# A new written-out order of the same instructions on all engines, and of the buffers they use (Mamba-2 SSD, then a SiLU feed-forward block)

## The chip, the cores and the metric

The kernel runs on one core of a Trainium2 chip. The metric is the time of one execution on the device in microseconds (us). An engine is named as in the profile: PE is TensorE, the matrix unit, and PEld its weight loads; DVE is VectorE, ACT is ScalarE, POOL is GpSimd, SP is SyncE, which only issues transfers here.

## The reference

Two stages run one after the other. The first is a chunked state-space scan over 4 batches x 8 heads of 768 steps, with 32 channels and 16 states per head; `a` is the decay of each step, `x`, `B` and `C` are the inputs. The second is a feed-forward block with SiLU on the result, seen as 3,072 tokens of 256 numbers.

```python
# scan, for each chunk; cum = cumsum(log a) within the chunk
M = einsum('bhin,bhjn->bhij', Cc, Bc) * exp(cum_i - cum_j) * causal
y = einsum('bhij,bhjd->bhid', M, xc) + einsum('bhin,bhnd->bhid', Cc, state) * exp(cum)
state = exp(sum(la)) * state + sum_j(Bc_j x xc_j * exp(cum_last - cum_j))
# feed-forward: x (3072, 256), w_in (256, 2048), w_out (2048, 256)
h = x @ w_in
out = (h / (1 + exp(-h))) @ w_out
```

## The kernel before, in words

**Tiling.** The sequence is cut into 12 units of 256 steps (three per batch, numbered `u` = 0 to 11), each worked as four chunks of 64 steps. Two units make a pair `G` of 512 tokens, on which the feed-forward block works. The 2,048 hidden features are 8 groups of 256 (`i` or `j`). Weight tile `n` is group n of `w_in` for n under 8 and group n - 8 of `w_out` above.

**Two ways to multiply.** Pair 0 is multiplied in plain fp32 (`s`, line 667, and `n`, line 735). Pairs 1 to 5 use the faster fp32r format with each operand split into a high part and two corrections, `h`, `l` and `d`, so three cheaper products stand in for one (line 776 for the first matmul, 757 for the second). The weights are first rounded on the device from their raw bits, by ACT, DVE and an integer addition on POOL, and then split; the last step of the split is a transfer that accumulates onto its destination, issued from POOL (line 322).

**The order is written out by hand.** `SCHEDULE` (lines 18 to 96) is a list of tokens. Each names a step and its indices, and a loop at the end of the kernel calls the steps in that order:

```python
for tok in line.split():
    f, *q = tok.split(",")
    DO[f](*map(int, q))
```

A step emits instructions for one engine, or a transfer. So the list fixes the order of instructions on every engine and in every queue, and each engine works through its own in that order; one that waits holds back all behind it on the same engine. Between engines only data and buffers order the work. `SLOTS` (lines 98 to 112) says which physical buffer each new tile takes, out of 49 small ones (`s2k`), 12 large ones (`r4k`), 7 for raw weights and split activations (`raw`) and 3 banks of PSUM (`hp`).

**The steps that the prediction speaks of.**

| token | engine, line | what it does |
|---|---|---|
| `z` | PE 404, 406 | dummy matmuls at the start |
| `ip`, `ia`, `ir`, `lw,n`, `Ln`, `Lt`, `Lx`, `La`, `Lp` | mostly SP 338 to 346, 277, 243, 251, 258, 218, 226 | loads of decays, raw weights, B and C (two layouts, tiles `bn` and `tbc`), x, and the tables `az` (to `ab`) and `ac` (to `pz`) |
| `AA`, `AD` | POOL 425, 431, 433 | clip the decays and write them to the tables `az` and `ac` in DRAM, which `La` and `Lp` read back broadcast |
| `ab,u,k`, `tp,u` | PE 467, 496 | transposes at the start |
| `E,u,k` | DVE 477 | scan that makes the decay matrix of half `k` of a unit |
| `P,u`, `P01` | DVE 449, 442 | scan of the prefix products |
| `T,u,i` | DVE 490 | transposes B (`bh`, i = 0) or C (`ct`, i = 1) |
| `ce,u`, `C,u` | ACT 511; POOL or DVE 516 | C for the two parities of heads; C times the prefix (`cw`) |
| `B,u` | POOL 485 | B times the decays to the chunk's end |
| `g0,u`, `gd,u` | PE 550, 536 | the products C B and B x, in the PSUM banks `ga` and `gb` |
| `b,u,c` | ACT 559 | evacuates the B x products |
| `M,u,w` | DVE 565 | C B times the decay matrix |
| `S,u,t`, `SM,u` | DVE 578, 580; ACT 588 | the state from chunk to chunk; its copy for the matmul |
| `Y,u` | PE 601, 610 | the unit's output: within the chunk (needs `M`), from the state (needs `SM` and `cw`) |
| `y`, `xh`, `x,u,0`, `x,u,1` | ACT 643, 649; DVE 624, 627 | evacuate `Y` and split it into `h`, `l`, `d` |
| `u,n`, `v,n`; `w,n,*`; `W,n` | ACT 283, 286; DVE 292, 296, 299; POOL 310 | round weight tile n |
| `H`, `Wl`, `Wd`; `Wm`, `We` | ACT 314, 318; POOL 322 | split weight tile n; the accumulating transfers for its `l` and `d` |
| `s,u,j`, `si`; `n` | PE 667, ACT 673; PE 735 | first and second matmul of pair 0 |
| `a,G,i`, `ax`, `d,G,i`, `dg` | PE 776, ACT 787, PE 776, ACT 797 | first matmul of pair G: `h` and `l` products, a scaling, `d` product, SiLU |
| `h`, `l`, `e` | ACT 803, DVE 624, 627 | split the result |
| `f,k` | PE 757 | the next k matmuls of the second product, from a list that `e` fills (12 per group) |
| `Va`, `Vd`, `Vt`, `o`, `O`, `ot`, `or`, `os` | ACT, DVE, PE, SP 763, 769, 697, 685, 689, 709, 715, 717, 720 | evacuate, transpose and store a pair |

The buffers that tie units together: `ab` and `xt` exist twice (unit u and u + 2 share one), `pz`, `tbc`, `bn`, `pfx`, `ct`, `bh`, `ce`, `cw` and `sm` once. `ga` and `gb` serve `g0`, `gd`, `Y` and, in turn, the first matmul of the pairs (even groups `ga`, odd ones `gb`).

## Time and profile before

| | us |
|---|---|
| runs of the kernel before | 335.66, 335.91, 340.67; median 335.91 |
| the profiled execution | 338.26, of which its span 336.4 |
| busy: PE, DVE, ACT, POOL | 322.3, 226.6, 216.6, 79.9 |
| idle time of PE with a named wait | 10.2 in eleven waits, the longest 1.8 |
| bytes moved by the DMA engines | 35.03 MB, mean 104 GB/s |
| DMA share by 8-us stretches, 8 to 40 and 80 to 104 us (no unit) | 0.96 to 1.14 |

The span is the time from the first to the last instruction of the profiled execution; the rest of its time lies around it. Durations below come from this one execution, and sums are made against it. A busy engine is one with an instruction in flight: a matmul's end is modelled, so busy PE time may hold small pauses, which show only in the times from start to start. Idle time of an engine other than PE costs nothing by itself; it matters where PE waits for what that engine has not yet done. A DMA share is the mean busy share of the core's 16 DMA engines, and can read a little over 1 in a short stretch.

### The profile page before, as it was taken

The page shows a single profiled execution, that of the slowest core. Times are in us where ns is not written, and L with a number is a line of the kernel's source. Part 1 is how long each engine was busy: PE and PEld are TensorE (multiplying, and loading weights), DVE is VectorE, ACT ScalarE, POOL GpSimd, SP SyncE. Part 2 cuts the span into 40 slices and gives each one's busy share as a digit, 9 for nine tenths or more (in the row PEclk, how much of TensorE's full clock was granted, in tenths as well). Part 3 has the DMA queues.
Part 4 walks back from the last instruction along what each step waited for, and adds up shares of the span by engine and source line. Part 5 has one row for each costly group of instructions (what it writes and reads, how often), then busy time and mean ns, then how long its engine had stood idle before and what let it go on. Part 6 is the DMA issues. An engine that isn't in the chain of part 4 may idle for free.

```text
span 336.4 us, 7603 instructions
## 1 busy us (share of the span) xinstructions
PE 322.3 (96%) x3086; PEld 245.5 (73%) x3086; DVE 226.6 (67%) x314; ACT 216.6 (64%) x340; POOL 79.9 (24%) x96
## 2 busy tenths in 40 slices
PE   7799999988999999999999999999999999999994
PEld 3578746664667878886887888778887888888883
DVE  4995998569525974858596499775656933737473
ACT  3589988674599777574763775655667655375431
POOL 2286765828451641100030020000000000000000
PEclk9999999999799999999999999999999999999998
DMA  7999869997998896232342162262000320004002
GB/s 182 180 323 255 222 152 256 231 172 134 236 189 133 160 188 111 71 56 37 80 104 51 25 144 43 43 126 35 2 0 2 55 33 2 0 0 72 0 0 62
DMA packets 98129, 35.03 MB, mean 104 GB/s; under 512 B 80352, under 2 KB 87264, under 8 KB 98096
## 3 DMA queue, kind: packets, MB, share of 16 engines
q1 hardware_dynamic: 90960, 25.71, 34.4%
q0 software_dynamic: 4784, 8.59, 14.1%
q10 hardware_dynamic: 2352, 0.26, 0.5%
q8 instruction: 24, 0.39, 0.5%
q14 instruction: 9, 0.07, 0.1%
HBM read 22.81 MB, written 3.34 MB: 78 GB/s over the span
## 4 chain that ended last, share of the span: by engine, by line
PE 82%; DVE 7%; SPq 4%; DMA 4%; issue 2%; ACT 1%; POOL 0%; ACTq 0%; DVEq 0%; POOLq 0%
PE hp L757 27%; PE gb L776 16%; PE ga L776 16%; PE o_ps L757 5%; PE hp L667 5%; PE hp L735 5%; DMA tbc<-in_B_dram 3%; DVE ab L477 2%; PE ga L610 1%; DVE st L580 1%; PE ga L601 1%; PE ga L550 1%; SPq L251 1%; PE ga L536 1%; DVE ab L565 1%
## 5 line engine op out<-in xcount | busy, mean ns | idle before, releaser
L757 PE MATMUL hp<-r4k,s2k 128*128 128x512 f32 x400 | 112.4, 393 | 0.0
L757 PEld LDWEIGHTS hp<-r4k,s2k 128*128 128x128 f32 x400 | 74.4, 188 | 16.3 <-issue 0.3
L624 DVE SCALAR_TENSOR_TENSOR r4k<-r4k,r4k 128x1024 fp32r<-128x1024 f32 x40 | 49.5, 1240 | 31.1 <-ACT r4k L803 30.0
L627 DVE SCALAR_TENSOR_TENSOR r4k<-r4k,r4k 128x1024 fp32r<-128x1024 f32 x40 | 48.5, 1218 | 31.3 <-ACT r4k L803 21.6
L776 PE MATMUL ga<-raw,s2k 128*128 128x512 f32 x240 | 62.7, 396 | 2.0 <-ACT r4k L673 1.2
L776 PE MATMUL gb<-raw,s2k 128*128 128x512 f32 x240 | 61.7, 392 | 0.0
L776 PEld LDWEIGHTS ga<-raw,s2k 128*128 128x128 f32 x240 | 44.8, 188 | 13.9 <-issue 1.6
L776 PEld LDWEIGHTS gb<-raw,s2k 128*128 128x128 f32 x240 | 44.7, 188 | 10.5 <-ACT gb L787 0.6
L803 ACT ACTIVATE r4k<-r4k 128x1024 fp32r<-128x1024 f32 x40 | 41.5, 1054 | 0.5 <-DVE r4k L627 0.4
L322 POOL DMA_DIRECT2D s2k<-s2k x32 | 31.4, 1206 | 30.5 <-ACT s2k L318 12.0
L787 ACT ACTIVATE ga<-ga 128x1024 f32<-128x1024 f32 x20 | 20.2, 1010 | 22.6 <-PE ga L776 22.6
L787 ACT ACTIVATE gb<-gb 128x1024 f32<-128x1024 f32 x20 | 20.2, 1010 | 22.2 <-PE gb L776 22.2
L735 PE MATMUL hp<-r4k,s2k 128*128 128x512 f32 x64 | 31.5, 628 | 0.0
L757 PE MATMUL o_ps<-r4k,s2k 128*128 128x512 f32 x80 | 31.0, 393 | 0.0
L797 ACT ACTIVATE r4k<-ga 128x1024 f32<-128x1024 f32 x20 | 20.5, 1025 | 16.2 <-PE ga L776 15.6
L667 PE MATMUL hp<-r4k,s2k 128*128 128x256 f32 x128 | 29.6, 383 | 0.0
L310 POOL TENSOR_TENSOR s2k<-s2k,s2k 128x512 uint32<-128x512 uint32 (+1 forms) x19 | 27.4, 1454 | 6.3 <-DVE s2k L296 4.3
L667 PEld LDWEIGHTS hp<-r4k,s2k 128*128 128x128 f32 x128 | 23.8, 190 | 4.9 <-issue 0.9
L485 POOL TENSOR_TENSOR BT<-bn,ab 128x256 f32<-128x256 f32 x10 | 9.0, 899 | 74.5 <-DVE ab L477 58.3
L477 DVE TENSOR_TENSOR_SCAN ab<-ab,diag 128x512 f32<-128x512 f32 x20 | 25.1, 1257 | 0.0
L797 ACT ACTIVATE r4k<-gb 128x1024 f32<-128x1024 f32 x20 | 20.5, 1025 | 5.6 <-PE gb L776 3.8
L735 PEld LDWEIGHTS hp<-r4k,s2k 128*128 128x128 f32 x64 | 12.4, 199 | 12.8 <-issue 11.3
(118 smaller groups left out, 385.3 us busy)
## 6 DMA issues: line engine op xcount, KB each, us to landing
s2k<-s2k POOLq DMA_DIRECT2D x32, 256.0 KB, 6.2
ab<-az SPq DMA_DIRECT2D x20, 256.0 KB
raw<-in_moe_w_in_dram SPq DMA_DIRECT2D x8, 512.0 KB
raw<-in_moe_w_out_dram SPq DMA_DIRECT2D x8, 512.0 KB
out_dram<-r4k SPq DMA_DIRECT2D x44, 64.0 KB
xt<-in_x_dram SPq DMA_DIRECT2D x20, 128.0 KB
pz<-ac SPq DMA_DIRECT2D x10, 130.0 KB
bn<-in_B_dram SPq DMA_DIRECT2D x20, 64.0 KB
```

The source lines that it names most:

```text
L310: nc.gpsimd.tensor_tensor(out=dst[:, :, fs].bitcast(U32), in0=u[:, :, fs], in1=v[:, :, fs], op=ALU.add)
L322: nc.gpsimd.dma_start(out=f32(WK[n, p]).rearrange("p k f -> p (k f)"), in_=other.rearrange("p k f -> p (k f)"), accum_op=ALU.add)
L477: nc.vector.tensor_tensor_scan(out=o, data0=src, data1=diag.rearrange("p h t -> p (h t)"), initial=0.0, op0=ALU.mult, op1=ALU.add)
L624: nc.vector.scalar_tensor_tensor(out=l, in0=f32(h), scalar=BACK, in1=y, op0=ALU.mult, op1=ALU.add)
L627: nc.vector.scalar_tensor_tensor(out=d, in0=f32(h), scalar=-(BACK + 1.0), in1=y, op0=ALU.mult, op1=ALU.subtract)
L667: nc.tensor.matmul(out=hp[:, i], lhsT=WT[j][:, kc, 128 * i:128 * i + 128], rhs=XM[:, 2 * kc:2 * kc + 2, u], start=(kc == 0), stop=(kc == K ...
L735: nc.tensor.matmul(out=NP["o"][m], lhsT=WT[8 + f // 2][:, f % 2, 128 * m:128 * m + 128], rhs=GT[0, f // 2][:, f % 2], start=(f == 0), stop ...
L757: nc.tensor.matmul(out=ACC[P, 2 * (p == "d") + m], lhsT=WK[8 + f // 2, p][:, f % 2, 128 * m:128 * m + 128], rhs=rhs, start=(f == 0 and p ! ...
L776: nc.tensor.matmul(out=o, lhsT=WK[j, q][:, kc, 128 * i:128 * i + 128], rhs=xs[:, 2 * kc:2 * kc + 2], start=(start and q == "h" and kc == 0 ...
L787: nc.scalar.activation(t, t, AF.Copy, scale=1.0 + Z)
L797: nc.scalar.activation(g, t, AF.Silu, scale=BACK)
L803: nc.scalar.activation(t, GT[G, i], AF.Copy, scale=-LESS * Z)
```

## The change

Only `SCHEDULE` and `SLOTS` change: all 77 lines of the first and the lists of the second. Every step is still called once with the same indices, except that the `n` and `f` steps are cut into other portions. The code of the steps is the same, and so are the line numbers. The order was searched for with a model of the engines and transfers; it was found with transfers of two queues sharing the DMA engines, and GpSimd's early dispatch of its next instruction, in the model. The diff below shows the lines around the places that the prediction speaks of: the start, units 2 and 3, unit 4, unit 7, and the buffer lists.

```diff
-ch ci Ln,0,0,0,1 ip,0,0 cI Ln,0,0,1,1 c1 cp cP ia,1 z,1 z,1 z,1 P01,0,0 P01,0,1 z,0,6 lw,0 z,0,6 z,0,6 ia,0 A
-ab,1,1 Ln,1,0,0,0 ce,0,1 ip,1,0 B,0,1 Ln,1,0,1,0 E,0,0 v,2 E,1,1 Ln,1,1,1,0 Lx,1,1,0 B,0,0 ce,0,0 tp,0 D,0 S,0,0 w,2,0
-tq,0 ir,0 g0,0 Lx,1,0,0 S,0,1 ab,1,0 M,0,1 tp,1 ce,1,0 ce,1,1 lw,1 S,0,2 tq,1 E,1,0 SM,0,1 ir,2 C,0 M,0,0 P01,1,0
-w,2,2 lw,4 SM,0,0 B,1,1 B,1,0 w,2,1 Y,0 X0,0,0 X0,0,1 W,2,2,0 P01,1,1 S,0,3 w,0,2 D,1 S,1,0 W,2,2,1 u,1 W,0,2,0 g0,1
...
-s,0,3 w,9,1 si,1,4 W,8,1,0 Wd,1 H,3 s,1,3 ce,2,0 Lp,2,0 w,11,0 w,10,1 AD,1 n,1 W,10,1,0 si,0,3 v,5 E,2,0 n,1 T,3,1
-H,4 M,2,0 W,11,1,0 Wd,4 P,2 b,2,0 Ln,3,0,1,0 Wl,0 w,7,2 H,9 n,1 b,2,1 Lx,3,0,0 S,2,0 Lt,3,0,1,0 w,7,1 n,1 u,6 Lp,3,0
-S,2,1 M,2,1 W,5,1,0 s,0,5 C,2 Lt,3,0,2,0 S,2,2 Ln,3,0,0,0 Lx,3,1,0 Wl,2 SM,2,0 v,6 SM,2,1 w,6,0 Wm,0 E,3,0 u,12 n,1
...
-w,13,2 u,13 Wm,11 Lt,5,1,0,0 xh,3 x,3,0 We,0 s,1,5 W,12,1,0 w,13,0 n,2 Wm,3 T,4,0 ce,4,0 Wm,9 si,1,5 Wl,5 a,1,0 v,15
-E,4,0 E,4,1 x,3,1 u,15 w,15,2 Wd,8 Lp,4,0 We,3 ax,1,0 s,1,7 B,4 ce,4,1 d,1,0 Lx,4,0,0 H,12 Ln,5,0,1,0 S,3,3 n,1 si,1,7
-n,1 w,13,1 dg,1,0 P,4 g0,4 Lt,5,1,3,0 w,14,2 W,13,1,0 gd,4 n,1 H,6 La,5,1,0 n,2 b,4,0 Lt,5,1,2,0 M,4,1 M,4,0 C,4 S,4,0
-w,14,1 Wd,11 b,4,1 S,4,1 We,4 Wd,9 S,4,2 SM,4,1 SM,4,0 Y,4 We,2 Wm,5 y,4,0 n,1 y,4,1 Ln,5,0,0,0 W,14,1,0 Lx,5,0,0 H,7
...
-f,1 Vd,1,0 Lt,8,1,2,0 Vd,1,1 B,7 f,1 Lx,7,1,0 f,2 dg,2,2 f,2 g0,7 gd,7 e,2,1 b,7,0 f,1 M,7,0 Lt,8,0,2,0 T,8,1 f,1
-Lx,8,0,0 Ln,8,0,1,0 x,6,0 ce,8,1 f,1 b,7,1 f,2 o,1,0,2 f,1 h,2,2 f,1 M,7,1 a,2,4 Lx,8,1,0 S,7,0 S,7,1 ax,2,4
...
+ch ip,0,0 cI ci z,1 z,1 z,1 Ln,0,0,0,1 P01,0,0 Ln,0,0,1,1 z,0,6 z,0,6 z,0,6 lw,0 ia,0 c1 z,1 ia,1 cp z,1 z,1 z,1 z,1
+Ln,1,1,0,0 tq,0 ab,1,1 ce,0,1 lw,1 ce,0,0 g0,0 Ln,1,1,1,0 B,0,1 v,2 E,1,1 ip,1,0 ir,3 B,0,0 v,1 D,0 ab,1,0 C,0
+Lx,1,0,0 u,1 w,2,0 tp,1 S,0,0 B,1,1 Lt,3,1,0,0 M,0,1 ce,1,1 E,1,0 S,0,1 Lx,1,1,0 M,0,0 S,0,2 SM,0,1 w,2,1 w,2,2 SM,0,0
+B,1,0 tq,1 P01,1,0 Y,0 S,0,3 P01,1,1 D,1 ce,1,0 S,1,0 w,0,2 w,1,0 X0,0,0 lw,3 X0,0,1 lw,10 W,2,2,0 lw,4 S,1,1
+Lt,3,1,2,0 S,1,2 g0,1 M,1,1 ir,0 W,2,2,1 ir,1 s,0,2 w,1,1 M,1,0 ir,2 lw,9 Lt,3,1,1,0 W,0,2,0 w,1,2 lw,8 Lt,3,1,3,0
+W,0,2,1 u,3 co s,0,0 v,3 SM,1,1 C,1 SM,1,0 S,1,3 Ln,2,1,0,0 si,0,2 Y,1 w,3,0 u,10 W,1,2,0 v,4 W,1,2,1 Ln,2,1,1,0
...
+W,3,1,0 s,0,4 AA,1 H,4 si,0,4 ca Lx,3,1,0 lw,11 La,2,0,0 w,9,1 s,1,4 tp,2 Lt,3,0,1,0 w,8,1 u,5 s,1,3 si,0,1 Lt,3,0,3,0
+Wd,2 W,8,1,0 si,1,4 Lx,2,1,0 v,10 n,1 tq,2 si,1,3 w,5,0 AD,0 v,5 n,1 u,11 n,1 ce,2,1 E,2,1 W,9,1,0 n,1 v,6 H,8 n,1
+v,11 lw,7 w,5,1 Lx,2,0,0 AD,1 H,1 ce,2,0 E,2,0 w,5,2 B,2 Lt,3,0,2,0 w,11,0 Lt,4,1,1,0 n,1 s,0,3 u,7 v,7 g0,2 u,6
+Lp,2,0 Wl,0 w,7,0 w,10,2 W,10,1,0 gd,2 W,5,1,0 Wl,4 P,2 w,11,1 H,3 La,3,1,0 La,3,0,0 b,2,0 n,1 C,2 n,1 E,3,0
+Ln,3,0,0,0 n,1 si,0,3 lw,15 S,2,0 ce,3,1 b,2,1 w,11,2 Wl,3 S,2,1 lw,12 M,2,0 Wl,8 H,10 Lt,3,0,0,0 s,0,5 lw,14 Wd,8 H,5
+M,2,1 n,1 S,2,2 Wl,10 w,7,1 si,0,5 Wm,0 SM,2,1 E,3,1 Wd,5 W,11,1,0 n,2 Lt,4,1,0,0 SM,2,0 H,9 Wl,2 Y,2 Ln,3,0,1,0
+Lp,3,0 w,7,2 W,7,1,0 We,0 w,6,0 Lx,3,0,0 u,12 La,4,0,0 lw,13 n,1 y,2,1 Wd,4 Wl,1 B,3 w,6,1 Wm,1 T,3,0 ce,3,0 Wm,4
...
+s,1,5 x,2,1 E,4,0 Ln,4,0,0,0 Ln,4,0,1,0 y,3,1 y,3,0 S,3,3 xh,3 x,3,0 a,1,0 x,3,1 Wl,9 si,1,5 ax,1,0 T,4,1 w,15,0 E,4,1
+n,2 Lx,4,1,0 u,13 We,1 ce,4,0 H,12 B,4 Wm,5 w,13,2 w,14,2 w,13,0 Lp,4,0 T,4,0 w,14,0 d,1,0 w,13,1 ce,4,1 Wl,11 w,14,1
+n,1 dg,1,0 s,1,7 Wd,3 g0,4 gd,4 M,4,1 W,13,1,0 Wm,9 P,4 Wd,12 Lt,5,1,0,0 h,1,0 W,14,1,0 Lx,5,0,0 b,4,0 La,5,1,0 si,1,7
+C,4 Lt,5,0,0,0 AD,2 b,4,1 M,4,0 n,1 S,4,0 Lt,5,1,2,0 S,4,1 S,4,2 Wl,7 n,3 Wd,7 SM,4,0 Lp,5,0 n,1 We,8 SM,4,1 Y,4 y,4,0
...
+g0,7 b,7,0 P,7 Lt,8,0,0,0 f,1 Lt,8,1,0,0 M,7,0 f,1 b,7,1 h,2,2 f,1 h,2,3 M,7,1 f,1 Lt,8,1,3,0 f,1 S,7,0 Ln,8,0,0,0
+l,2,1 e,2,2 S,7,1 f,2 a,2,4 f,1 Lt,8,0,3,0 Lt,8,0,1,0 f,2 Lt,8,0,2,0 Lx,8,1,0 T,8,0 C,7 ax,2,4 a,2,5 ax,2,5 l,2,2
...
 SLOTS = {
     "s2k": """
-7 10 19 30 2 22 4 5 8 26 6 0 3 1 9 11 12 13 14 15 16 17 18 20 21 23 24 25 27 28 29 31 32 33 34 35 36 37 38 39 40
...
+4 11 23 35 0 22 3 6 8 27 7 1 5 2 9 10 12 13 14 15 16 17 18 19 20 21 24 25 26 28 29 30 31 32 33 34 36 37 38 39 40
...
     "raw": """
-0 1 2 3 4 5 6 1 0 2 3 4 6 1 5 2 6 3 0 4 0 5 1 2 6 3 0 4 5 1 2""",
+0 1 2 3 4 5 6 1 0 2 6 3 5 1 2 4 6 3 0 1 2 4 5 6 3 0 1 2 4 6 5""",
     "hp": """
-0 1 2 0 1 2 0 2 1 0 2 1 0 2 1 0 1 2 0 1 2 2 2 2 2 2 2 1 0 2 0 1 2 0 1 2 0 1 2 0 1""",
+0 1 2 0 1 2 2 0 1 2 1 0 2 0 2 0 2 1 0 2 2 2 2 2 2 2 2 0 1 2 1 0 2 1 0 1 0 2 1 0 2""",
```

## The prediction

> **What bounds the kernel now.** I read the page first: the span, the busy times and the granted clock over the 40 slices.

> ```profile
> span 336.4 us, 7603 instructions
> PE 322.3 (96%) x3086; PEld 245.5 (73%) x3086; DVE 226.6 (67%) x314; ACT 216.6 (64%) x340; POOL 79.9 (24%) x96
> ...
> PEclk9999999999799999999999999999999999999998
> ```

> TensorE (PE) is busy 96% of the span, VectorE (DVE) and ScalarE (ACT) about two thirds each, and one slice near 85 us runs at a lower clock. Every engine issues the same instructions in a new order, so the work of TensorE cannot shrink; only its pauses can move. I added up that work: 128 matmul records of L667 at 0.216 us, 64 of L735 at 0.43, 480 each of L757 and L776 at 0.227 (start to start, read off the timeline), and for each sequence unit about 2.4 us of small matmuls (L536, L550, L601, L610). From the first L667 at 19.12 us to the last L757 at 330.7 this gives 298.6 us of work in 311.6 us, so about 13 us are pauses or slow clock. Some 4 of these are 0.1-us hitches, most of them between small and large matmuls, which stay in any order.

> The waits of TensorE come next. Each row gives engine, tile, line, what it waited for, and then total us, times, longest.

> ```profile
> PE ga L601 <- DVE ab L565: 1.8, 1, 1.8
> PE ga L610 <- ACT sm L588: 1.7, 1, 1.7
> PE ga L536 <- issue: 1.3, 1, 1.3
> ...
> PE ga L776 <- ACT r4k L673: 1.2, 1, 1.2
> PE ga L776 <- ACT bxs L559: 0.7, 1, 0.7
> ```

> The first is the start of the kernel (16.4 us). The other four are the whole of what a new order could win after that, and the timeline says why three of them occur.

> ```profile
> 61.57 10.05 DMA tbc<-in_B_dram
> ...
> 71.64 0.66 DVE L490 STREAM_TRANSPOSE bh<-tbc 128x256 f32<-128x256 f32 x1 [2.07 <-DMA tbc<-in_B_dram]
> 72.14 2.28 DVE L477 TENSOR_TENSOR_SCAN ab<-ab,diag 128x512 f32<-128x512 f32 x2
> 74.34 0.67 DVE L627 SCALAR_TENSOR_TENSOR raw<-raw,ys 128x512 fp32r<-128x512 f32 x1
> ```

> (First line from the chain of work that ended last, the others from the timeline.) Here VectorE stands at `T,4,0` until a 10-us transfer lands, then does both scans `E,4`, and only then `x,3,1` (L627), which TensorE's `d,1,0` needs. TensorE idles from about 73.7 to 75.1 (the wait names ACT, but this operand came last).

> ```profile
> 80.59 2.77 DVE L580 SCALAR_TENSOR_TENSOR st<-st,pfx,bxs 128x64 f32<-128x64 f32 x2
> 80.99 2.27 POOL L310 TENSOR_TENSOR s2k<-s2k,s2k 128x512 uint32<-128x512 uint32 x1
> 83.39 0.69 ACT L588 ACTIVATE sm<-st,par 128x128 f32<-128x128 f32 x2 [2.44 <-DVE st L580]
> ```

> The second of the two small updates `S,4,1` and `S,4,2` lasts until GpSimd's addition `W,14` (L310) ends; the same form takes 0.28 us elsewhere. So `SM,4` is late, and `Y,4` stops TensorE for 1.7 us. Right behind it the clock drops.

> ```profile
> 83.00:84.00 1.00, 0.00 (x0) 0.00 (x0) 0.97 (x3) 0.61 (x2) 1.00 (x3) 1.00 1.19 249
> ...
> 86.00:87.00 1.00, 1.00 (x2) 0.34 (x1) 0.00 (x0) 0.97 (x3) 1.00 (x2) 0.50 1.11 252
> ```

> (Columns: stretch, its length, busy us of PE, PEld, DVE, ACT, POOL, then clock, DMA share, GB/s.) The L735 matmuls from 84.9 to 88.8 start 0.35 to 0.43 us later than their 0.43 rhythm, about 2.2 us in all.

> **The change part by part.** All counts per engine are unchanged (2,111 program rows on PE, 316 on DVE, 345 on ACT, 101 on POOL, 227 on SP), so nothing is added or removed; every term is a wait.

> *Start, 0 to 25 us.* The chain to `Y,0` is the same. One more dummy matmul (0.43 us) stands ahead of `ab,0,1`, which puts the first scan 0.4 us later; `S,0,2` now stands behind `M,0,0`, which gives back about 0.1. In `Y,1`, `C,1` now stands behind `w,1,2`, 0.68 us later, with little cover: about 0.5. Sum +0.8; bounds 0 (other work in front is also lighter) and +1.5.

> *Units 2 and 3, 36 to 60 us.* This is the part that the trace of before cannot show. The `ac` table of unit 2 (`AD,0`) moves behind `AA,1`, `W,3` and `W,8` on GpSimd; before, it was issued at 27.5. `W,8` needs `w,8,1`, which VectorE reaches at about 33 to 36 (it had done as much work by 35.9 before). So `AD,0` is issued at 36 to 38 and lands at 41 to 43 (the page's 4.6 us for `ac<-r4k`). SP stands at `Lp,2` until then, with `La,3,1` and `La,3,0` behind it (2 x 256 KB), and VectorE stands at `P,2` and then `E,3,0` for them. I take 44 to 46 for `P,2`. Behind it come `w,11,1`, `C,2`, `E,3,0`, three `S`, `w,11,2`, two `M`, `w,7,1`, `E,3,1`, `w,7,2`: 7.9 us by their rows, 6.9 with the 0.08 us by which neighbours overlap, 1.6 for two GpSimd additions that hold VectorE up, then `W,7` on GpSimd (1.5). That is 10.0 us to `s,0,7`, which TensorE reached at 54.56 and, with the same work in front, reaches at 55.4 now. So `P,2` may start as late as 45.4. I take +0.5; bounds 0 and +5.7 (below).

> *`x,3,1`.* In the new order it stands ahead of `T,4,1`, `E,4,1` and `T,4,0`. The sum of VectorE's rows in front of it falls from 47.8 to 44.4 us; `d,1,0` comes only 0.9 us earlier in TensorE's work. The wait of 1.4 us goes: -1.4. What is late next is `E,4,0`, which now stands in front of `x,2,1`'s followers and waits for `La,4`; that is issued once `Y,2` has ended (about 54), and 10 us to land, as in the row above, still ends at 64, when VectorE gets there.

> *`Y,4` and the clock.* 5.3 us of TensorE's work now lie between `g0,4` and `Y,4`, against 3.6 before. VectorE needs `M`, `P`, `M` and three `S` in that time, 2.9 us, and ACT 0.7. `W,13` and `W,14` still run there and may hold VectorE for up to 2.3 us. I count the 1.7 as gone but leave +0.5 for that: -1.2. With the pause the slow clock goes: -2.2. Bounds for the two: 0 and -3.9. [...]

> *`a,2,4`, 155.7 us.* The evacuation `b,7,1` stood on ACT behind `ce,8,1`, which waited for `T,8,1` on VectorE. Now `b,7,1` follows `b,7,0`, and `M,7,1` follows `M,7,0`. The pause of 1.1 us goes: -1.1.

> *Weights.* `lw,4` moves behind `lw,3` and `lw,10` (1 MB), `w,4,0` and `w,4,1` behind nine other VectorE steps; `W,4` then ends at about 31.4, `s,0,4` needs it at 32.4. The accumulating transfers (L322) land 6.2 us after issue; the one with the least time, `We,4` behind `W,15`, is issued at about 84, and `d,1,4` comes at about 99. Both hidden: 0; if the 1 us at `s,0,4` is gone, up to +1.

> *The hitch at 58.4 us* (1.3 us, "issue", inside `gd,3`) has no releaser in the profile. I leave it: 0; bounds -1.3 and +1.3.

> *The other 170 us.* The order of the large matmuls differs by at most 4 us of work anywhere. Before had one pause there; I allow +0.6 for new ones, bounds 0 and +2.

> The tail is the same chain of L697, L709, L717 and L720 with the same 18 matmuls behind `e,5,7`: 0.

> Sum: +0.8 +0.5 -1.4 -1.2 -2.2 -1.1 +0.6 = **-4.0 us**. The profiled execution took 338.26 us with a span of 336.4; it would become 334.3. It is 2.35 us above the median of the runs, 335.91, so the predicted median is 331.9, say **332**.

> **The rivals.**

> *The late table.* If `Lp,2` or `La,3` needs 10 us to land (the row of `tbc<-in_B_dram`) after an issue at 41, `P,2` or `E,3,0` starts at 51 and `s,0,7` at 61.0 in place of 55.4: 5.7 us, and a pause of that kind brings the half clock, 2.2 more. In place of the +0.5 that is +7.9: -4.5 + 7.9 = +3.4, so 339.3. It decides from `P,2` later than 45.4, and the kernel gets slower than before from about 48. For it: the DMA engines are busy at 0.75 to 1.1 in these 20 us, and one issue of `pz` took 4.6 us. Against it: before used the same bytes in the same time, and SP has 0.35 MB less to carry before `Y,2` than it had.

> *Given back to the DMA engines.* Summed over the stretches of the windows up to 128 us, the DMA engines are busy 119 us. If units 5 to 7 are paced by their loads, TensorE runs ahead by 4 us and waits for them: only the 1.1 at 155.7 and about 1 more stays, some 334.5 to 336. For it: VectorE already waited 2.7 us for `ab<-az` at 96.4. Against it: TensorE had no wait between 89 and 153 us, and shares of 0.49 at 72 to 80 and 0.66 at 104 to 112. This is also the case in which the two effects that the order was searched with are not those that held TensorE.

> *More than forecast.* Start at 0, the hitch gone, `Y,4` free: -1.4 -1.7 -2.2 -1.1 -1.3 = -7.7, so 328.2.

> **How the numbers follow.** Forecast (329.3 to 334) 0.50; given back or cancelled (334 to 337.5) 0.22; late table 0.18, half of it dearer than worked out because VectorE is full there and later units follow; more than forecast 0.10. Within 2% (6.7 us, about what a measurement of this kernel can tell from no change) lie 329.2 to 342.6. Faster by over 2%: 0.10. Slower by over 2%: 0.13, from the dearer part of the late table and pauses that I have not seen. Within: 0.77. The range is 328.5 to 340.5: it takes in the late table's price and most of the larger gain.

> **What would show it.** Right: no wait of L776 for `x,3,1` near 73 and of `sm` near 82, clock 1.0 from 80 to 90, no pause at 156, and `a,1,2` at about 83 to 85 in place of 88.8. The late table: VectorE idle before L449 or L477 between 43 and 52 with a DMA as releaser, and TensorE waiting at L610 or L667 near 55. Given back: waits of VectorE for `ab<-az` or `tbc` between 80 and 130 with TensorE idle behind them. The prediction is wrong if a pause of over 2 us opens anywhere that I counted as unchanged, above all if the clock falls with it.

## The result, and the profile after

The changed kernel takes 333.95 us (median of 20 runs, 330.77 to 336.51); the kernel before, run beside it, 339.8 us (20 runs, 335.17 to 342.09). The ratio is 0.988, interval 0.984 to 0.992: a little faster, inside the 2% that the prediction called "within". The forecast was 332.0 us against 335.91, a ratio of 0.988 too. (The ratios here count only the runs of a kernel within 1.5% of its fastest; the medians count all.) The three runs shown before were a low draw: in 120 runs of the kernel before, taken in the course of this study, the median was 339.2 us and the standard deviation 2.6. By medians the change brings 5.9 us, 1.7%. The profiled execution took 332.88 us in place of 338.26: -5.4, where the sum said -4.0.

The head of the changed kernel's page (span; busy time, share and instructions of each engine; granted clock in 40 slices; shares of the chain that ended last):

```profile
span 330.8 us, 7604 instructions
PE 320.5 (97%) x3086; PEld 245.9 (74%) x3086; DVE 227.7 (69%) x314; ACT 217.2 (66%) x340; POOL 76.7 (23%) x96
...
PEclk9879999999999999999999999999999999999998
...
PE 95%; DVE 1%; DMA 1%; SPq 1%; ACT 0%; issue 0%; ACTq 0%; DVEq 0%
```

The drop near 85 us is gone; two stretches at half clock stand at the start of the kernel, in the second and third slices (7.9 to 11.3 us and 18.2 to 21.6 us). TensorE is 95% of the chain (82% on the page of before), so almost nothing else is left on it. The waits of TensorE, the same view as before:

```profile
PE ga L601 <- DVE ab L565: 1.8, 1, 1.8
PE o_ps L416 <- DVE s2k L412: 1.5, 1, 1.5
PE o_ps L404 <- DVE s2k L351: 1.4, 1, 1.4
PE ga L550 <- ACT ce L511: 0.8, 1, 0.8
PE gb L709 <- DVE r4k L697: 0.5, 1, 0.5
```

Four of the waits that were shown of before are gone: `sm` at L610, the "issue" at L536, and L776 for `r4k` and for `bxs`. What remains is the start of the kernel (the first four rows, all in the first 30 us) and the tail (the last row); between them no wait with a named releaser is left. Around unit 4 (timelines of VectorE, GpSimd and ScalarE in the changed kernel: start, duration, engine, line):

```profile
69.40 0.68 DVE L627 SCALAR_TENSOR_TENSOR raw<-raw,ys 128x512 fp32r<-128x512 f32 x1
...
73.96 0.64 DVE L490 STREAM_TRANSPOSE bh<-tbc 128x256 f32<-128x256 f32 x1
...
77.17 1.59 POOL L310 TENSOR_TENSOR s2k<-s2k,s2k 128x512 uint32<-128x512 uint32 x1
...
79.84 1.04 DVE L580 SCALAR_TENSOR_TENSOR st<-st,pfx,bxs 128x64 f32<-128x64 f32 x3
80.92 0.69 ACT L588 ACTIVATE sm<-st,par 128x128 f32<-128x128 f32 x2 [1.39 <-DVE st L580]
```

`x,3,1` (L627) runs at 69.4 in place of 74.3, `T,4,0` at 74.0 with no wait in front of it. GpSimd's addition ends at 78.8, ahead of the three `S` updates, which take 1.04 us together, and `sm` is written from 80.9. TensorE starts `Y,4` at 81.85 without a pause, and the clock stays (windows, columns as before):

```profile
80.00:84.00 4.00, 4.00 (x104) 2.32 (x102) 2.88 (x6) 1.28 (x4) 4.00 (x6) 1.00 0.68 134
84.00:88.00 4.00, 4.00 (x17) 2.76 (x16) 0.00 (x0) 2.73 (x6) 3.94 (x5) 1.00 1.11 214
```

**Where the time went.** To add this up I give each execution a lateness: the start of a step's first matmul, minus the durations of all TensorE work that stands in front of it in that kernel's order, at the rates of the prediction. It grows only where TensorE pauses or runs slowly. The first column is the lateness at the first `s` of the second half (`s,1,0`), each next one its growth up to the step named, all in us of the profiled execution.

| execution | start | to `a,1,0` | to `d,1,0` | to `Y,4` | to `a,1,2` | to `g0,7` | to `a,2,4` | to `a,5,0` | sum |
|---|---|---|---|---|---|---|---|---|---|
| before | 7.0 | 1.9 | 1.8 | 0.4 | 3.2 | 1.6 | 1.1 | 2.4 | 19.3 |
| changed | 8.3 | 0.6 | -0.1 | 0.7 | -0.2 | 2.1 | 0.1 | 2.3 | 13.8 |
| b_b71 | 8.9 | 0.5 | 6.9 | 1.8 | 0.3 | 1.5 | 0.2 | 2.3 | 22.3 |
| b_x31 | 9.3 | 0.4 | 0.2 | 5.9 | -0.1 | 2.3 | 1.1 | 2.4 | 21.5 |
| b_t40 | 6.7 | 1.3 | 5.6 | 2.4 | 0.2 | 1.5 | 1.1 | 2.4 | 21.1 |
| b_three | 8.4 | 0.6 | 0.3 | 1.4 | -0.3 | 1.6 | 0.2 | 2.3 | 14.4 |
| b_w14 | 10.1 | 0.4 | 6.5 | 2.3 | -0.3 | 3.1 | 1.1 | 2.4 | 25.5 |
| b_lt | 8.4 | 0.4 | 0.9 | 0.4 | 1.6 | 1.6 | 1.1 | 2.3 | 16.6 |
| b_thin | 7.3 | 0.4 | 0.3 | 0.5 | 3.2 | 1.5 | 1.1 | 2.4 | 16.6 |
| b_lw | 8.1 | 0.5 | 1.2 | 0.4 | 1.6 | 1.5 | 1.1 | 2.4 | 16.8 |
| b_five | 10.4 | 1.7 | 0.2 | 0.5 | 0.0 | 3.2 | 0.2 | 2.3 | 18.5 |
| a_p2 | 6.9 | 1.6 | -0.1 | 0.7 | -0.3 | 1.7 | 0.2 | 2.4 | 13.1 |
| a_t40 | 10.2 | 0.6 | -0.1 | 0.7 | -0.2 | 3.1 | 0.1 | 2.4 | 16.8 |
| a_lw | 7.0 | 0.7 | -0.1 | 0.7 | -0.3 | 3.4 | 0.1 | 2.3 | 13.8 |

The names from the third row on are the experiments below (`b_` starts from before, `a_` from the changed kernel). Changed minus before gives -5.5, the -5.4 of the profile. The start differs from execution to execution of one and the same order by nearly 4 us, and no experiment touches it, so single executions must be read column by column, and times by their medians. With ten to twelve runs and a standard deviation near 2 us, a median is known to some 0.8 us, so a term of 1 us is seen in the columns and hardly in the times. The column "to `g0,7`" varies too, from 1.5 to 3.4 in executions of both orders, and no experiment explains it.

### The profile page after: what moved, and what is told of

The parts are those of the page before. It is cut to its first block, busy times and chain, and to the rows that moved or that the text cites. A ratio compares the mean times of both kernels' runs of the same rounds, so it can differ in the third digit from the quotient of the medians.

```text
span 330.8 us, 7604 instructions
## 1 busy us (share of the span) xinstructions
PE 320.5 (97%) x3086; PEld 245.9 (74%) x3086; DVE 227.7 (69%) x314; ACT 217.2 (66%) x340; POOL 76.7 (23%) x96
## 4 chain that ended last, share of the span: by engine, by line
PE 95%; DVE 1%; DMA 1%; SPq 1%; ACT 0%; issue 0%; ACTq 0%; DVEq 0%
PE hp L757 28%; PE ga L776 17%; PE gb L776 17%; PE hp L667 9%; PE hp L735 9%; PE o_ps L757 6%; PE ga L550 2%; PE ga L610 2%; PE ga L601 2%; PE gb L601 1%; PE ga L536 1%; DMA s2k<-in_a_dram 1%; PE gb L550 1%; PE hp L467 1%; DVE ab L565 0%; PE gb L610 0%
## 5 line engine op out<-in xcount | busy, mean ns | idle before, releaser
L757 PE MATMUL hp<-r4k,s2k 128*128 128x512 f32 x400 | 112.5, 393 | 0.0
L757 PEld LDWEIGHTS hp<-r4k,s2k 128*128 128x128 f32 x400 | 74.4, 188 | 16.3 <-issue 0.5
L776 PE MATMUL ga<-raw,s2k 128*128 128x512 f32 x240 | 62.8, 397 | 0.0
L776 PE MATMUL gb<-raw,s2k 128*128 128x512 f32 x240 | 62.5, 396 | 0.0
L627 DVE SCALAR_TENSOR_TENSOR r4k<-r4k,r4k 128x1024 fp32r<-128x1024 f32 x40 | 49.0, 1230 | 17.7 <-ACT r4k L803 8.6
L776 PEld LDWEIGHTS ga<-raw,s2k 128*128 128x128 f32 x240 | 44.7, 188 | 11.5 <-issue 1.0
L776 PEld LDWEIGHTS gb<-raw,s2k 128*128 128x128 f32 x240 | 44.7, 188 | 11.3 <-issue 1.2
L322 POOL DMA_DIRECT2D s2k<-s2k x32 | 29.5, 1207 | 18.2 <-DMA s2k<-s2k 11.6
L757 PE MATMUL o_ps<-r4k,s2k 128*128 128x512 f32 x80 | 31.3, 397 | 0.0
L735 PE MATMUL hp<-r4k,s2k 128*128 128x512 f32 x64 | 30.4, 600 | 0.0
L667 PE MATMUL hp<-r4k,s2k 128*128 128x256 f32 x128 | 30.3, 388 | 0.0
L477 DVE TENSOR_TENSOR_SCAN ab<-ab,diag 128x512 f32<-128x512 f32 x20 | 24.4, 1221 | 7.6 <-DMA ab<-az 7.6
L667 PEld LDWEIGHTS hp<-r4k,s2k 128*128 128x128 f32 x128 | 24.4, 194 | 6.5 <-issue 2.2
L797 ACT ACTIVATE r4k<-gb 128x1024 f32<-128x1024 f32 x20 | 20.5, 1026 | 10.8 <-PE gb L776 8.0
L310 POOL TENSOR_TENSOR s2k<-s2k,s2k 128x512 uint32<-128x512 uint32 (+1 forms) x19 | 24.0, 1273 | 15.5 <-DVE s2k L299 9.3
L318 ACT ACTIVATE s2k<-s2k 128x512 fp32r<-128x512 f32 x32 | 19.4, 629 | 0.0
```

The costliest lines, as they stand in the source:

```text
L310: nc.gpsimd.tensor_tensor(out=dst[:, :, fs].bitcast(U32), in0=u[:, :, fs], in1=v[:, :, fs], op=ALU.add)
L322: nc.gpsimd.dma_start(out=f32(WK[n, p]).rearrange("p k f -> p (k f)"), in_=other.rearrange("p k f -> p (k f)"), accum_op=ALU.add)
L477: nc.vector.tensor_tensor_scan(out=o, data0=src, data1=diag.rearrange("p h t -> p (h t)"), initial=0.0, op0=ALU.mult, op1=ALU.add)
L627: nc.vector.scalar_tensor_tensor(out=d, in0=f32(h), scalar=-(BACK + 1.0), in1=y, op0=ALU.mult, op1=ALU.subtract)
L667: nc.tensor.matmul(out=hp[:, i], lhsT=WT[j][:, kc, 128 * i:128 * i + 128], rhs=XM[:, 2 * kc:2 * kc + 2, u], start=(kc == 0), stop=(kc == K ...
L735: nc.tensor.matmul(out=NP["o"][m], lhsT=WT[8 + f // 2][:, f % 2, 128 * m:128 * m + 128], rhs=GT[0, f // 2][:, f % 2], start=(f == 0), stop ...
```

## The experiments

Theory: three places in the order of the steps held TensorE up, VectorE's at `x,3,1` and at `S,4`, ScalarE's at `b,7,1`; with each step moved, its share of the gain appears. Rival: the loads of unit 4 land late whatever stands in front, because the DMA engines are full, so moving steps on VectorE moves the loss.

**One part alone, and all three.** Each is the kernel before with one step moved.

```diff
# b_w14: w,14,1 behind the state updates and their copies
-S,4,0 w,14,1 Wd,11 b,4,1 S,4,1 We,4 Wd,9 S,4,2 SM,4,1 SM,4,0 Y,4
+S,4,0 Wd,11 b,4,1 S,4,1 We,4 Wd,9 S,4,2 SM,4,1 SM,4,0 w,14,1 Y,4
# b_x31: x,3,1 ahead of T,4,0 and the scans
-Wm,3 T,4,0 ce,4,0 Wm,9 si,1,5 Wl,5 a,1,0 v,15 E,4,0 E,4,1 x,3,1 u,15
+Wm,3 x,3,1 T,4,0 ce,4,0 Wm,9 si,1,5 Wl,5 a,1,0 v,15 E,4,0 E,4,1 u,15
# b_b71: b,7,1 ahead of ce,8,1
-x,6,0 ce,8,1 f,1 b,7,1 f,2
+x,6,0 b,7,1 ce,8,1 f,1 f,2
# b_three: all three moves
```

> The kernel before with one step moved: w,14,1 (VectorE, L296) stands behind SM,4,0, so that the addition W,14 on GpSimd (L310) can only start behind S,4,1 and S,4,2. Theory (the addition stretched the small updates, that made the pause at Y,4, and the pause made the slow clock): the two S take about 0.3 us each in place of 2.77 together, the wait of L610 for sm (1.7 us) is gone, the clock stays at 1.00 from 80 to 90 us, a,1,2 starts at about 85.0 in place of 88.8, and the execution is 3.9 us shorter. Rival 1 (the slow stretch does not hang on the pause): the clock is 0.50 somewhere between 80 and 90 all the same, and only 1.7 us are won. Rival 2 (W,14 is late now): a new wait of L776 opens between 90 and 110 us and the gain is given back. In the part before 60 us nothing is changed: if the hitch of 1.3 us inside gd,3 near 58 us belongs to this order, it is there again.

> The kernel before with x,3,1 (VectorE, L627) moved ahead of T,4,0, nothing else. Theory: the wait of L776 in d,1,0 (1.4 us near 73.5) is gone, d,1,0 starts at about 73.7 in place of 75.1, and TensorE stays 1.4 us ahead: -1.4 us. Rival (Y,4 is paced by the transfer tbc that lands at 71.6, by T,4,0 and by the scans behind it, which do not come earlier): TensorE reaches Y,4 1.4 us earlier and waits 1.4 us longer there (3.1 us in place of 1.7), and nothing is won, or, if the longer pause lengthens the slow clock, up to 1.7 us is lost. The hitch inside gd,3 near 58 us is there again if it belongs to this order.

> The kernel before with b,7,1 (ACT, L559) moved ahead of ce,8,1, nothing else. Theory: the wait of L776 in a,2,4 near 155.7 us (1.1 us between the 757 and the 776 matmuls) is gone and nothing takes its place: -1.1 us in the profile, too little for the times. Rival: ce,8,1 comes no later, but M,7,1 behind T,8,1 holds the other bank, so the wait moves on to a,2,5 and 0.5 us or more of the 1.1 stays. The hitch inside gd,3 near 58 us is there again if it belongs to this order.

> The kernel before with the three single moves together (w,14,1 behind SM,4,0; x,3,1 ahead of T,4,0; b,7,1 ahead of ce,8,1). Theory (three pauses with three causes of their own): the gains add, 3.9 + 1.4 + 1.1 = 6.4 us, so the profile is as short as that of the changed kernel or shorter (about 330 to 332.5 us), though only three of about 1,400 steps are moved. Rival (Y,4 is paced by the load and not by TensorE): the 1.4 us come back as a pause at Y,4, -5.0 us at most, and the slow clock can return with it (-2.8).

Measured, beside a before of 340.5 us: b_w14 340.9 (ratio 1.007, 1.001 to 1.013), b_x31 340.7 (0.998, 0.995 to 1.002), b_b71 340.0 (1.001, 0.995 to 1.007). Not one of them gains what its term said in the times. b_three gives 334.9 (0.979, 0.972 to 0.987), but in four runs only, one of which is still at 340.1. The trace of b_b71, which differs from before only at 156 us, shows what hides the single gains (timeline of VectorE, then windows):

```profile
77.15 0.64 DVE L490 STREAM_TRANSPOSE bh<-tbc 128x256 f32<-128x256 f32 x1 [7.16 <-DMA tbc<-in_B_dram]
77.64 2.27 DVE L477 TENSOR_TENSOR_SCAN ab<-ab,diag 128x512 f32<-128x512 f32 x2
79.83 0.67 DVE L627 SCALAR_TENSOR_TENSOR raw<-raw,ys 128x512 fp32r<-128x512 f32 x1
```

```profile
72.00:76.00 4.00, 2.29 (x11) 1.64 (x9) 0.00 (x0) 2.42 (x4) 0.86 (x1) 1.00 1.27 217
76.00:80.00 4.00, 0.00 (x0) 0.00 (x0) 2.85 (x4) 0.00 (x0) 0.00 (x0) 0.59 0.58 110
```

The same chain as in the profile of before, but the load of `tbc` lands 5.5 us later: VectorE stands 7.2 us, TensorE does nothing from 76 to 80 us, and the granted clock falls (mean 0.59 in these 4 us, 0.56 in the next). The column "to `d,1,0`" is 6.9 here and 1.8 in the first profile of before: this one place differs from execution to execution by more than the whole forecast. At `a,2,4` b_b71 has 0.2 in place of 1.1, so that term is right, and too small for a median to show.

In b_x31, `x,3,1` no longer waits, and the loss appears one step further (timelines of VectorE and TensorE):

```profile
74.95 0.70 DVE L490 STREAM_TRANSPOSE bh<-tbc 128x256 f32<-128x256 f32 x1 [4.02 <-DMA tbc<-in_B_dram]
...
80.99 5.49 PE L735 MATMUL hp<-r4k,s2k 128*128 128x512 f32 x6 [1.63 <-POOL s2k L310]
```

`d,1,0` is in time (0.2), but 5.9 us go before `Y,4`: VectorE stood 4 us at `T,4,0`, the `n` matmuls wait for an addition on GpSimd behind it, and the clock is halved from 80.28 to 87.11. Moving `x,3,1` alone does not save the time. b_three's profiled execution had its load at 72.45, and the three columns are as the theory has them (0.3, -0.3, 0.2), with 1.4 up to `Y,4`, 0.8 of it the same wait for the addition.

**Does the place of `T,4,0` matter at all?** It was tried from both sides, with the load of its last tile issued earlier as a third test.

```diff
# b_t40: before, T,4,0 behind the scans and x,3,1
-Wm,3 T,4,0 ce,4,0 Wm,9 si,1,5 Wl,5 a,1,0 v,15 E,4,0 E,4,1 x,3,1 u,15
+Wm,3 ce,4,0 Wm,9 si,1,5 Wl,5 a,1,0 v,15 E,4,0 E,4,1 x,3,1 T,4,0 u,15
# a_t40: the changed kernel, T,4,0 back ahead of x,3,1
-a,1,0 x,3,1 Wl,9 ... w,13,0 Lp,4,0 T,4,0
+a,1,0 T,4,0 x,3,1 Wl,9 ... w,13,0 Lp,4,0
# b_lt: before, the load Lt,4,0,3 ahead of La,4,0
-La,4,0,0 ... La,4,1,0 Lt,4,0,3,0
+Lt,4,0,3,0 La,4,0,0 ... La,4,1,0
```

> The kernel before with T,4,0 (VectorE, L490) moved behind E,4,0, E,4,1 and x,3,1, nothing else. In the profiles so far with the order of before, T,4,0 started at 71.6, 77.2 and 77.9 us, each time when its load landed, and TensorE stood at d,1,0 for 1.4, 6.3 and 5.9 us. Theory (VectorE standing at T,4,0 in front of x,3,1 is what makes the kernel before slow and uneven): no wait of L776 at d,1,0; a landing as late as 78 costs only the 1 to 2 us by which g0,4 is late; no slow clock between 76 and 85; the times lose their upper half (most below 339) and the median falls by 3 to 4 us. Rival (the load ab of E,4,1, 256 KB, issued right before on the same queue, lands just as late): VectorE now waits at L477 for ab<-az as long as it did at L490, x,3,1 behind it is as late, and the times stay as they are.

> The changed kernel with T,4,0 put back ahead of x,3,1, nothing else. Theory (the place of T,4,0 on VectorE is the core of the gain): x,3,1 waits for the landing of tbc, somewhere from 70 to 75 us; d,1,0, which starts at 72.3 in the profile of the changed kernel, comes 0 to 3 us later from one execution to the next, in some with 1.7 us of slow clock; median +1 to +3 us, and a wider spread. Rival (the changed order also issues these loads earlier, so that they have landed before VectorE gets there): no wait at L490, no change over 0.5 us.

> The kernel before with the load Lt,4,0,3 (SP, L251, 32 KB, the last piece that T,4,0 waits for) issued ahead of La,4,0 and La,4,1 in place of behind them. Theory (all loads of this stretch share DMA engines that are busy at 1.0 to 1.2 from 52 to 76 us, so that what stands last is late): T,4,0 starts by 68, but then L477 waits for ab<-az until 70 to 77; x,3,1 stands behind it, and the times change by less than 2 us. Rival (only the tbc pieces are slow): T,4,0 and both E,4 are done by 71, d,1,0 does not wait, and the gain is that of T,4,0 moved behind x,3,1, 3 to 4 us in the median.

Measured: b_t40 336.9 beside 338.4 (0.999, 0.995 to 1.003; 1.6 us less by medians), b_lt 338.4 (0.997, 0.992 to 1.002), a_t40 333.8 (0.990, 0.987 to 0.993), that is, no loss against the changed kernel. In b_t40 VectorE waited all the same, now for the table `ab`, which comes on the same queue (timeline of VectorE):

```profile
74.98 2.34 DVE L477 TENSOR_TENSOR_SCAN ab<-ab,diag 128x512 f32<-128x512 f32 x2 [6.28 <-DMA ab<-az]
77.24 0.67 DVE L627 SCALAR_TENSOR_TENSOR raw<-raw,ys 128x512 fp32r<-128x512 f32 x1
```

In a_t40, which puts `T,4,0` back ahead of `x,3,1` in the changed kernel (`E,4,1` stays behind it), neither waits:

```profile
71.25 0.69 DVE L490 STREAM_TRANSPOSE bh<-tbc 128x256 f32<-128x256 f32 x1
71.78 0.69 DVE L627 SCALAR_TENSOR_TENSOR raw<-raw,ys 128x512 fp32r<-128x512 f32 x1
```

The theory on VectorE's order at `x,3,1` falls here: `T,4,0` ahead of `x,3,1` makes no loss where the load is there (a_t40), and `x,3,1` ahead of `T,4,0` takes none away where it is late (b_x31). What differs is when the loads land.

**Is it the bytes?** b_thin leaves 1 MB of weight loads out and keeps before's order.

```diff
# b_thin, in load_w
+if n >= 14:
+    raw[n] = raw[12]
+    return
# b_lw: before, the same 1 MB earlier instead of left out
-u,6 Lp,3,0 S,2,1 ... Lt,3,0,0,0 lw,14 lw,15 ct Y,2
+u,6 lw,14 lw,15 Lp,3,0 S,2,1 ... Lt,3,0,0,0 ct Y,2
# a_lw: the changed kernel, 1.5 MB later, right ahead of unit 4's first load (two raw buffers swapped)
-E,3,0 ... lw,15 ... lw,14 ... u,12 La,4,0,0 lw,13
+E,3,0 ... u,12 lw,15 lw,14 lw,13 La,4,0,0
```

> The kernel before in its own order, with the loads of the raw weight tiles 14 and 15 (2 x 512 KB) left out; their weights are made from tile 12 instead, so the output is not the reference's, and all other instructions stay. Theory (the loads of unit 4 land late because 1.5 MB of raw weights stand in front of them while the DMA engines are full): 1 MB at the 230 to 250 GB/s of that stretch is about 4 us, so L490 for bh and L477 of unit 4 start about 4 us earlier than the 71.6 to 77.9 seen with the order of before; the wait at d,1,0 is 0 to 2 us in place of 1.4 to 6.3; the median falls by 3 to 5 us and the spread shrinks. Rival (bytes do not matter, the small packets or VectorE's order do): the landing is where it was, and the times change by less than 1 us.

> The kernel before with the two loads lw,14 and lw,15 (1 MB) issued ahead of Lp,3, where SP stands still for 1.7 us, in place of behind the loads of unit 3; nothing else. Theory (the DMA engines are not full from 44 to 52 us, at shares of 0.5 to 0.9, so a megabyte moved there clears the way for unit 4): L477 of unit 4 starts 2 to 4 us earlier, the wait at d,1,0 shrinks as much, and the median falls by 2 to 4 us. Rival (the loads of unit 3 are now the late ones): L490 or L536 of unit 3 wait 2 to 4 us near 55 to 60 us, TensorE with them, and the gain is given back: 0, or up to 2 us slower.

> The changed kernel with the three loads lw,15, lw,14 and lw,13 (1.5 MB of raw weights) issued right ahead of La,4,0, as the kernel before has them, and the two raw buffers named to suit; nothing else. Theory (that these stand further ahead is the core of the gain): La,4 and the pieces of tbc land 3 to 5 us later, E,4,0 on VectorE (L477, 66.2 us in the profile of the changed kernel) waits for ab<-az, x,3,0 and x,3,1 behind it are late, TensorE waits 2 to 5 us at a,1,0 or d,1,0, the clock falls in some executions; the median rises by 2 to 5 us, to that of the kernel before or near it, and the spread with it. Rival (the gain is spread over many places): less than 1 us.

Measured, beside 338.0: b_thin 335.2 (0.995, 0.992 to 0.999), b_lw 337.3 (1.004, 1.000 to 1.007), a_lw 333.5 (0.991, 0.988 to 0.994). In b_thin's timeline of VectorE `T,4,0` comes at 68.2 without a wait (its lines are 3 higher than in before):

```profile
68.24 0.65 DVE L493 STREAM_TRANSPOSE bh<-tbc 128x256 f32<-128x256 f32 x1
...
70.92 0.67 DVE L630 SCALAR_TENSOR_TENSOR raw<-raw,ys 128x512 fp32r<-128x512 f32 x1
```

The wait at `d,1,0` is gone with the bytes (0.3), the median falls by 2.8 us, and the standard deviation from 2.4 to 0.8 us: the spread of before goes with that load. (b_x31 has a small spread as well, 0.9, but at 340.7 us: none of its ten runs is below 338.9, and eight of the 25 of before beside it are.) `Y,4` and `a,2,4` stay (3.2 and 1.1), as they should. So before's main loss is a transfer that lands late behind other transfers. But its timing is not one move's doing: 1 MB issued earlier brings 0.7 us by medians (b_lw), and 1.5 MB put back does the changed kernel no harm (a_lw). Where the two orders differ before that is seen in the windows of 48 to 52 us, of before and of the changed kernel:

```profile
48.00:52.00 4.00, 4.00 (x15) 2.38 (x14) 4.00 (x10) 3.02 (x8) 2.27 (x2) 1.00 0.50 97
```

```profile
48.00:52.00 4.00, 4.00 (x15) 2.56 (x14) 3.99 (x9) 3.94 (x9) 2.27 (x3) 1.00 1.06 317
```

Before leaves the DMA engines half empty there in this execution (share 0.50, 97 GB/s); the executions with the loads where before has them carry 89 to 169 GB/s in these 4 us, at shares of up to 0.92, and the changed kernel carries 317. From 64 to 72 us both have them full (shares 1.18 and 1.20, and 1.22 and 1.15), so what was not carried earlier is what before still has in front of `tbc`. Of SP's loads 10.3 to 10.5 MB had landed by 52 us in the executions of before's order, 10.8 to 11.5 MB in those of the changed one. That goes with the result; but b_lw, with 11.1 MB, still lost 1.2 us at `d,1,0`, so bytes landed by 52 us are not the whole rule.

Part of the lateness arises before the transfer begins. SP issues the last piece of `tbc` for `T,4,0` at 61.57 us in before and at 69.19 in b_b71, which starts 1.9 us later. The issues in front of it take SP longer there: that of `La,4,1`, the last in front, holds it for 1.57 us in the first and 4.36 in the second (timelines of SP, before and b_b71):

```profile
59.95 1.57 SPq L218 DMA_DIRECT2D ab<-az  x1
61.57 0.68 SPq L251 DMA_DIRECT2D tbc<-in_B_dram  x1
```

```profile
64.78 4.36 SPq L218 DMA_DIRECT2D ab<-az  x1
69.19 1.19 SPq L251 DMA_DIRECT2D tbc<-in_B_dram  x1
```

Less the lateness of the start (first column), this piece is issued at 50.9 to 52.0 us in the four executions of the changed order and its variants, at 53.0 in b_thin, and at 54.6 to 60.3 in the eight others that issue it behind `La,4,1` as before does. Most of what it shares the DMA engines with is not SP's: from 64 to 81 us of b_b71 GpSimd's accumulating transfers (queue q0) move 1.86 MB and SP's loads (q1) 1.20 MB (queue, packets, MB, share of the 16 engines):

```profile
q0 software_dynamic: 1029, 1.86, 62.7%
q1 hardware_dynamic: 4779, 1.20, 37.2%
```

No run moves these transfers by themselves, so how much of the lateness is theirs is not shown.

**Moves that should suffice.** b_five has six moves: the three of b_three, `T,4,0` behind the scans, and `lw,14` and `lw,15` as in b_lw.

> The kernel before with six steps moved: w,14,1 behind SM,4,0; x,3,1 ahead of ce,4,0; T,4,0 behind E,4,1; b,7,1 ahead of ce,8,1; the loads lw,14 and lw,15 ahead of Lp,3. Theory (the gain of the changed kernel comes from the late loads of unit 4, the pause at Y,4 with its slow clock, and the pause at a,2,4, and from nothing else in its 1,400 steps): all three are gone in every execution, the median is 333 to 335 us, as that of the changed kernel, no run is above 337, and the runs lie within about 4 us. Rival (a late load still has other ways to TensorE, or other parts of the new order carry a good share): a run near 340 is still among them, or the median stays above 336.

Measured: 337.6 beside 340.6, -3.0 by medians, half of the gain (0.999, 0.994 to 1.004). The three pauses are gone (0.2, 0.0, 0.2), but the moved 1 MB has a price: VectorE waits for unit 3's C (timeline), and 1.7 us go before `a,1,0` in place of some 0.4; 3.2 go up to `g0,7`, and the start of this execution is also the latest of all.

```profile
61.20 0.65 DVE L490 STREAM_TRANSPOSE bh<-tbc 128x256 f32<-128x256 f32 x1 [2.38 <-DMA tbc<-in_C_dram]
```

**How far the late table was.** In a_p2 the two tables of unit 3 are issued ahead of `Lp,2`, so `P,2` must wait behind 512 KB more.

```diff
-g0,2 u,6 Lp,2,0 Wl,0 ... P,2 w,11,1 H,3 La,3,1,0 La,3,0,0 b,2,0
+g0,2 u,6 La,3,1,0 La,3,0,0 Lp,2,0 Wl,0 ... P,2 w,11,1 H,3 b,2,0
```

> The changed kernel with the load Lp,2 (SP, L226) issued behind La,3,1 and La,3,0 in place of ahead of them, which makes P,2 late on purpose: the late table of the prediction. Theory (by the sum of the prediction, P,2 may start as late as 45.4 us; it started at 44.9 in the profile of the changed kernel): P,2 starts at 47 to 50, s,0,7 comes later by the same less 0.5, so TensorE waits 1.5 to 4.5 us somewhere between Y,2 and s,0,7, and half the clock for 3.4 us adds up to 1.7: +2 to +6 us. Rival (the chain behind P,2 has more slack than worked out): TensorE waits less than 1 us, no change that the times show.

Measured: 333.3 in four runs, the changed kernel's time (0.989, 0.984 to 0.994). `P,2` comes at 46.39 after a wait of 2.79 us, in an execution that starts 1.4 us earlier than the changed one, whose `P,2` stands at 44.91:

```profile
46.39 0.70 DVE L449 TENSOR_TENSOR_SCAN pfx<-pz,one 128x260 f32<-128x260 f32 x1 [2.79 <-DMA pz<-ac]
```

That is 2.9 us later against TensorE's work; TensorE lost 1.0 (column "to `a,1,0`": 1.6 against 0.6), where the working of the prediction, with 0.5 us to spare, gives 2.4. There was more room than it found.

## Why the prediction was right, and where it was not

The direction, the size and the class were right: -4.0 forecast in the profiled execution and -5.4 measured, a ratio of 0.988 forecast and 0.988 measured. That the two ratios are equal is partly luck: by the medians of all runs the ratio is 0.983, and the gain of 5.9 us is half as much again as forecast. `a,1,2` starts at 83.87 us, forecast 83 to 85. 332.0 us itself lies 2 us low, since the runs it was scaled to were a low draw; scaled to the median of 20 it would have been 335.8 (339.8 - 4.0), 1.9 us high.

| term | forecast | profiled, changed minus before | what the runs say |
|---|---|---|---|
| start | +0.8 | +1.3 | no effect of the order seen: 8.4 on average in ten executions of before's start, 8.1 in four of the new one |
| units 2 and 3 | +0.5 | +0.2 | right; `P,2` at 44.9, forecast 44 to 46 |
| `x,3,1` | -1.4 | -1.9 | wrong cause, and 0.9 to 6.9 in the executions with `x,3,1` where before has it (b_thin aside) |
| `Y,4` and clock | -3.4 | -3.4 | right; with `w,14,1` moved -0.3 and 0.0 in place of 3.2 (b_three, b_five) |
| `a,2,4` | -1.1 | -0.9 | right; 0.2 in all with `b,7,1` moved, 1.1 in all others of before's order |
| hitch | 0 | -1.5 | one execution's; 0.1 to 0.4 in the same step of all the others |
| other | +0.6 | +0.7 | near it in this execution; 0.5 of it is "to `g0,7`", which differs by 1.9 between executions |

**The step that failed is "`x,3,1`".** The prediction read the wait as a matter of VectorE's order: "In the new order it stands ahead of `T,4,1`, `E,4,1` and `T,4,0`", so the wait goes. b_x31 makes that move and loses the time one step later; b_t40 takes `T,4,0` out of the way and VectorE waits for the scans' table instead; a_t40 puts `T,4,0` back ahead of `x,3,1` in the changed kernel and loses nothing. The line that decided it stood in the prediction: a 10-us transfer of `tbc`, at the head of the chain. Its landing was taken as given, when it is the thing that varies (`T,4,0` behind it starts at 71.6 to 77.9 us). It also cost more than 1.4 us where the load came late: 5.6 to 6.9 us in three executions (b_t40, b_w14, b_b71). For the same reason one rival had its effect the wrong way round: "given back to the DMA engines" feared that the shared DMA engines would take the gain back, but they are where before lost it, and from 68 to 80 us the changed kernel runs at shares of 0.80 to 1.15 with TensorE busy throughout (windows):

```profile
68.00:72.00 4.00, 4.00 (x17) 2.86 (x16) 3.21 (x6) 2.62 (x5) 2.62 (x3) 1.00 1.15 195
72.00:76.00 4.00, 4.00 (x16) 2.71 (x15) 3.51 (x8) 4.00 (x9) 2.49 (x3) 1.00 1.12 211
76.00:80.00 4.00, 4.00 (x72) 2.01 (x72) 2.77 (x4) 3.52 (x8) 3.29 (x4) 1.00 0.80 153
```

That transfers of both queues share the DMA engines is seen in the rows of b_b71 above: GpSimd's queue and SP's fill the same 16 engines together, 62.7% and 37.2% of their time. b_thin is no test of it, since the 1 MB left out stood in SP's own queue; it shows that with less in that queue `T,4,0` ran at 68.2 us in place of 71.6 to 77.9.

The sign that the prediction named for that rival does appear, without its price: between 80 and 130 us VectorE waits 5.7 us for `ab<-az` and 2.7 for `tbc<-in_C_dram` in the changed kernel, and TensorE does not wait behind it. In a_lw it does: two pauses, 1.1 us together, follow such a wait at 119 and 121 us.

**The terms do not simply add.** Where the load is late, the pause at `Y,4` is absent (b_b71: 6.9 and then 0.3), probably because TensorE comes there later while VectorE catches up. So before pays the late load or `Y,4` with its clock, or some of each, and an edit that cures one can leave the other: that fits the single moves, which gave nothing, and the three together, which gave most in four runs. How b_three does with a late load is not shown: its profiled execution had it at 72.45, and one of its runs is at 340.1. In b_w14 the cause of the pause at `Y,4` is moved away, and its profiled execution pays 6.5 us at `d,1,0`.

**The start** was forecast at +0.8 from the extra dummy matmul and `C,1`. In the changed execution the first scan is 0.1 us later, not 0.4, and `C,1` costs nothing; 0.4 us come from `D,0` behind `g0,0`, for which `S,0,0` waits 0.39 us, and the rest from a stretch of half clock. Averaged over the executions no difference is left.

**What stays open:** which of the many moves among the loads between 36 and 64 us makes unit 4's land in time. b_lw and a_lw show that the weight tiles' place alone does not, and b_five that they are not free to move. It may be several, each enough, and GpSimd's accumulating transfers, which the new order moves as well, may have a part. The late landing itself is shown (b_thin, b_t40); its control by the order of loads is inferred from the changed kernel, where the four profiled executions of its order and its variants issue the load earlier and none of them had the late landing.

## What to carry to other kernels

When a wait's releaser is a transfer, ask first why it lands when it does, from the moment its queue issued it and from the share of the DMA engines in the 10 us ahead of it, before costing the order of the steps that wait for it; here moving the waiting step only handed the wait to the next one. A spread of 3% between runs of one program can be the mark of such a wait, as it was here, so look at a second execution before sizing it. And test edits together as well as one by one: where two stalls cover each other, each cure alone can measure as nothing.

## What the runs showed of the hardware

```profile
81.88:85.30 3.42, 1.74 (x97) 1.39 (x81) 2.24 (x3) 1.05 (x4) 3.42 (x5) 1.00 1.17 238
85.30:88.71 3.41, 3.41 (x5) 1.35 (x4) 0.95 (x1) 2.92 (x6) 2.86 (x3) 0.50 1.12 227
```

```profile
78.75:82.17 3.42, 2.73 (x69) 1.27 (x67) 3.38 (x5) 0.86 (x3) 3.42 (x6) 1.00 1.11 195
82.17:85.58 3.41, 2.31 (x36) 1.45 (x37) 1.02 (x3) 2.25 (x6) 3.41 (x5) 1.00 1.16 243
85.58:88.99 3.41, 3.41 (x14) 2.36 (x13) 1.90 (x3) 2.08 (x4) 1.64 (x2) 1.00 1.14 225
```

With the whole pause in one stretch (TensorE busy 1.74 of 3.42 us, and 1.71 in b_thin) the next one runs at 0.50 and the place costs 3.2 us; split over two (2.73 and 2.31 busy here, 3.01 and 2.05 in b_lw) nothing drops and it costs 1.6. So the forecast's 2.2 us for the clock is luck of the phase as much as of the order. In the changed kernel the same happens at the start: a stretch with 1.50 us busy is followed by one at half clock (windows):

```profile
14.74:18.15 3.41, 1.50 (x91) 1.13 (x89) 3.41 (x9) 1.64 (x5) 0.59 (x2) 1.00 0.98 271
18.15:21.57 3.42, 3.42 (x82) 2.61 (x72) 3.28 (x8) 2.19 (x6) 2.79 (x4) 0.50 0.99 332
```

One pair of stretches speaks against a plain threshold: 13.62 to 17.03 in before, with 1.61 us busy, was followed by full clock, and 4.50 to 7.91 in the changed kernel, with 1.65, by half clock. What rule sets the clock is not shown. In before the pause ahead of the drop was 1.7 us, half of one stretch of the grid, and with `w,14,1` moved that place costs -0.3 and 0.0 us in place of 3.2 (b_three, b_five).

**A load on a queue named `instruction` landed just ahead of the hitch.** The trace of before has 24 loads of 16 KB on this queue. Which engine they serve is not shown; that it is TensorE is an estimate from the counts, 6,172 matmuls and weight loads among the 7,603 instructions of the page. In the profiled before one landed at 58.30, and the 1.3-us pause marked "issue" began at 58.41, inside `gd,3`; in b_b71 and b_x31 one landed 2.1 and 0.7 us before `g0,3` began, and there was no pause. That such a load made the hitch is argued from this one coincidence, not shown.
